# Early spectral weights loaded as row pairs, with two modes on partitions of opposite parity

## The chip, the cores and the metric

One Trainium2 chip, of which the kernel uses one core. The metric is device time in microseconds of one execution of the whole program. The core has TensorE (PE, matmuls), VectorE (DVE), ScalarE (ACT), GpSimd (POOL, which here mainly issues loads), SyncE (SP) and 16 DMA engines that carry every transfer between HBM and the on-chip SBUF. Matmul results land in PSUM, eight banks of 2 KB on each of 128 partitions.

## The reference

Attention with a forget gate, then a spectral mixing layer:

```
scores = (q @ k.T) / sqrt(64) + cum[i] - cum[j]      # cum = cumsum(log f), causal
attn   = softmax(scores);  x = attn @ v              # q, k, v: (8, 8, 576, 64) f32
x      -> (8, 576, 512)                              # heads side by side
X = rfft(x, axis=1)[:, :64]                          # 64 modes
Yr = Xr @ w_r - Xi @ w_i;  Yi = Xr @ w_i + Xi @ w_r  # per mode, w_r, w_i: (64, 512, 512) f32
y = irfft(Y, 576);  u = x + y
out = u + relu(u @ w_ch)                             # (8, 576, 512) f32
```

The two weight tensors are 134 MB together and each element is used once for each of eight batch entries. They are most of what is read.

## The kernel before

**The order.** The kernel is written under a manual schedule: each engine runs its instructions in program order. A loop of 34 turns does the attention of 32 items (four pairs of heads, `g`, by eight batch entries, `b`; item `i` is `pairs[i]`, so items 0 to 7 have `g` = 0, 8 to 15 have `g` = 1). A turn `i` holds, for item `i`, the transposes of q and k (`trans`), of v (`turn_v`, `back_v`), the scores and their exponentials on ScalarE (`scores`, lines 457 and 464), the masks; for item `i-1` the products with v (`av`, line 505) and the normalisation into `x_all` (`norm`, line 520); for item `i-2` the spectrum (`dft`). Behind the loop stands the weight stage: for each unit of four modes the remaining weight tiles are multiplied with the spectrum, and the inverse transform and the output product follow.

**The loads.** GpSimd issues q, k, v and the weights in one queue; the load casts f32 to bf16. Each turn `i` issues q and k of item `i+4`, half a weight tile (`issue_half`), v of item `i+3`, and, but in turns 3, 6, 9, 12 and 15 (`less`), another half. A weight tile has 1 MB (bf16): four modes of one unit `u`, and a quarter `dc` of the work of these modes. It sits in a rotating pool of seven buffers (`NW`), or, for a few early tiles (`guests`), in space that is not yet used. A tile's load must wait until the matmuls of the tile that had its buffer are done. The order is `wseq`: the 28 tiles of `early`, then the rest by unit.

**Two layouts of weights.** For the first eight units (`NL`, 32 modes `ML`) and the first 256 rows of the 512 (`dc` 0 and 1, 128 rows each), a tile holds w_r and w_i of four modes with one weight row on one partition (`by_rows`). One packet of such a load writes one row: 512 bf16 elements, 1 KB. In all other tiles one partition holds a pair of adjacent rows, `2p` and `2p+1`, so that one packet writes 2 KB; for the units from eight on, `dc` 0 is w_r and `dc` 1 is w_i of the first 256 rows, `dc` 2 and 3 the same of the last 256.

**The spectrum.** `dft` multiplies a block of `x_all` (time by 128 channels) with `bas3`, a basis of three planes (minus sine, cosine, sine; written by `setup_basis` in turn 1). A partition of the result is a channel. For `g` 0 and 1 it makes three groups of five matmuls: all 128 channels with the first 32 modes, which are copied to `XS`, and even channels and odd channels with the last 32 modes, on 64 partitions each, which are copied to `XQ` (by row pair). Both copies are on ScalarE (lines 543 and 547). For `g` 2 and 3 two groups make even and odd channels with all modes for `XP`.

**The early products.** `spec_early` multiplies the tiles of `early` inside the loop: two in each of turns 10 to 13, two in turn 17 behind `dft`, two in each of 18 and 19, and one in each turn from 20. `spec_mms` issues eight matmuls of 512 columns (line 221) for a tile, each with 32 (or 16) columns of spectrum as the stationary operand, and puts mode `j` into rows 32`j` to 32`j`+31 of the PSUM tile, so that four of them work on four column strips of the array. The result goes to `yacc` in `yx` by a ScalarE copy (`dc` 0) or a VectorE sum. In the weight stage `Yb` is brought to rows by a matmul with `perm`.

**PSUM.** `psM`, two buffers, is shared in order by the transposes, `pd` of `dft`, and the early products.

Of the kernel before, what the change touches and what calls it, by code (L numbers as in the profile page):

```python
# [10 lines left out]
F32 = mybir.dt.float32  # L11
BF16 = mybir.dt.bfloat16
I32 = mybir.dt.int32
ALU = mybir.AluOpType
ACT = mybir.ActivationFunctionType
# [8 lines left out]
def kernel(  # L24
# [11 lines left out]
    nc = tc.nc  # L36
    B, H, S, Dh = q.shape
    NM = moe_w_r.shape[0]
    D = H * Dh
    assert S == 576 and Dh == 64 and D == 512 and H == 8, (B, H, S, Dh)  # L40
    assert NM == 64 and B == 8
    NSB = 5
    SBLK = [128, 128, 128, 128, 64]
    NEB = D // 128
# [7 lines left out]
    NX = 12  # L52
    NL = 8
    ML = 4 * NL
    XROW = 24 * ML + 32
    scale = 1.0 / math.sqrt(Dh)
    TWO_PI_OVER_S = 2.0 * math.pi / S
    NEAREST = 1.5 * 2.0**23
# [5 lines left out]
    const = ctx.enter_context(tc.tile_pool(name="const", bufs=1))  # L64
    wpool = ctx.enter_context(tc.tile_pool(name="wpool", bufs=NW))

    yx = const.tile([128, 8, 1280], F32, name="yx")
    x_all = const.tile([128, NEB, B, NSB, 128], BF16, name="x_all")
    XS = const.tile([128, 2, XROW], BF16, name="XS")
    XP = const.tile([128, 2, 24, NM], BF16, name="XP")  # L70
    XQ = const.tile([128, 2, 24, NM - ML], BF16, name="XQ")
    wch = const.tile([128, NEB, D], BF16, name="wch")
    ident_bf = const.tile([128, 128], BF16, name="ident_bf")
    ident_f = const.tile([128, 128], F32, name="ident_f")
    trimask = const.tile([128, 128], BF16, name="trimask")
    tri4 = const.tile([128, 2, 64], BF16, name="tri4")
    perm = const.tile([128, 64], BF16, name="perm")
    Zt = const.tile([128, NSB, NM, 2], F32, name="Zt")
    bas3 = const.tile([128, NSB, 3, NM], BF16, name="bas3")
# [3 lines left out]
    wT = const.tile([128, NPAIR, 9], BF16, name="wT")  # L83
    wn = const.tile([128, NPAIR, 9], F32, name="wn")
    coef = const.tile([128, 1], F32, name="coef")
    accT = const.tile([128, NEB, B, 8], F32, name="accT")


    actx = ExitStack()
    ssb = actx.enter_context(tc.tile_pool(name="ssb", bufs=1))  # L90
# [10 lines left out]
    psM = actx.enter_context(tc.tile_pool(name="psM", bufs=2, space=PSUM))  # L101
# [44 lines left out]
    def by_rows(u, dc):  # L146

        return dc < 2 and u < NL

    def issue_w(half=None):  # L150
        n = wissued[0]
        if n >= len(wseq):
            return
        u, dc = wseq[n]
        if half != 1:
            if n in guests:
                t = 2 if by_rows(u, dc) else 4
                w8 = guests[n][:, 0 : 8 * D].rearrange("p (t m e) -> p t m e", t=t, e=D)
            else:
                shape = [128, 2, 4, D] if by_rows(u, dc) else [128, 4, 2, D]  # L160
                w8 = wpool.tile(shape, BF16, tag="w8", name="w8")
            wtile[(u, dc)] = w8
        w8 = wtile[(u, dc)]
        if by_rows(u, dc):
            for t, src in enumerate((moe_w_r, moe_w_i)):
                if half in (None, t):
                    nc.gpsimd.dma_start(
                        w8[:, t, :, :],
                        src[4 * u : 4 * u + 4, dc * 128 : (dc + 1) * 128, :].rearrange("m p e -> p m e"),
                    )  # L170
        elif dc < 2:
            src = (moe_w_r, moe_w_i)[dc]
            step = 4 if half is None else 2
            for j in range(2 * (half or 0), 4 if half != 0 else 2, step):
                m = 4 * u + j
                nc.gpsimd.dma_start(
                    w8[:, j : j + step, :, :].rearrange("p m r e -> p m (r e)"),
                    src[m : m + step, 0:256, :].rearrange("m (p r) e -> p m (r e)", r=2),
                )
        elif half != 1:  # L180
            src = (moe_w_r, moe_w_i)[dc - 2]
            step = 1 if n + 1 == len(wseq) else 4
            for j in range(0, 4, step):
                m = 4 * u + j
                nc.gpsimd.dma_start(  # L185
                    w8[:, j : j + step, :, :].rearrange("p m r e -> p m (r e)"),
                    src[m : m + step, 256:512, :].rearrange("m (p r) e -> p m (r e)", r=2),
                )
        if half != 0:
            wissued[0] += 1  # L190
# [7 lines left out]
    XPv = XP[:].rearrange("p r c m -> p (r c) m")  # L198
    XQv = XQ[:].rearrange("p r c m -> p (r c) m")

    def by_pair(dc, c, n, m):

        c0 = 24 * c + (8 if dc % 2 == 0 else 0)
        if dc < 2:
            return XQv[:, c0 : c0 + n, m - ML]
        return XPv[:, c0 : c0 + n, m]

    def spec_mms(A, u, dc, first, last):
        w8 = wtile.pop((u, dc))
        for n in range(2):  # L210
            for j in range(4):
                m = 4 * u + j
                st_, sp_ = first and n == 0, last and n == 1
                if by_rows(u, dc):
                    M = 32
                    c0 = m * 24 + (8 if n == 0 else 0)
                    lhsT, rhs = XS[:, dc, c0 : c0 + 32], w8[:, n, j, :]
                else:
                    M = 32 if st_ else 16
                    lhsT, rhs = by_pair(dc, n, M, m), w8[:, j, n, :]  # L220
                nc.tensor.matmul(  # L221
                    A[32 * j : 32 * j + M, :], lhsT=lhsT, rhs=rhs, start=st_, stop=sp_
                )

    def spec_cols(AT, dc, modes=range(4)):
# [19 lines left out]
    cum, ones1 = yx[:BH, 1, 0 : 2 * S + 64], yx[:BH, 5, 0:S]  # L245

    s_i = ssb.tile([128, NSB], I32, name="s_i")
    m_i = ssb.tile([128, 128], I32, name="m_i")
    nc.gpsimd.iota(s_i[:], pattern=[[128, NSB]], base=0, channel_multiplier=1)
    nc.gpsimd.iota(m_i[:], pattern=[[1, 128]], base=0, channel_multiplier=0)  # L250
    nc.sync.dma_start(ft, f.rearrange("b h s -> (b h) s"))
    for i in range(3):
        load_v(i, nc.sync)
# [8 lines left out]
    s_f = ssb.tile([128, NSB], F32, name="s_f")  # L262
    m_f = ssb.tile([128, 128], F32, name="m_f")
    nc.vector.tensor_copy(s_f[:], s_i[:])
    nc.vector.tensor_copy(m_f[:], m_i[:])
    nc.vector.tensor_scalar(ident_bf[:], m_f[:], s_f[:, 0:1], None, ALU.is_equal)
    nc.vector.tensor_scalar(s_f[:], s_f[:], float(S - 1), None, ALU.min)
    sm = tmpC.rearrange("p t s m -> p t (s m)")
# [61 lines left out]
        nc.vector.tensor_copy(tri4[64:128, 1, :], trimask[64:128, 64:128])  # L330

    def setup_basis():
        nc.vector.tensor_scalar(bas3[:, :, 0, :], Zt[:, :, :, 1], -1.0, None, ALU.mult)
        nc.vector.tensor_copy(bas3[:, :, 1, :], Zt[:, :, :, 0])
        nc.vector.tensor_copy(bas3[:, :, 2, :], Zt[:, :, :, 1])

    def setup_late():
        nc.vector.memset(XS[:, :, 24 * ML : XROW], 0.0)
        nc.vector.tensor_copy(
            perm[:].rearrange("p (b j ri) -> p b j ri", b=8, j=4),  # L340
            ident_bf[:].rearrange("p (j x ri b) -> p b j x ri", j=4, x=2, ri=2)[:, :, :, 0, :],
        )
        nc.vector.tensor_copy(rep[:], _strided(ident_bf[:, KF:128], [[0, 4], [1, KL]]))
        nc.gpsimd.dma_start(wch[:], moe_w_ch.rearrange("(eb p) e -> p eb e", p=128))
# [182 lines left out]
    def dft(i):  # L527
        g, b = pairs[i]
        if g < 2:
            pd = psM.tile([128, 3, 3, ML], F32, tag="m", name="pd")  # L530
            half = slice(64 * g, 64 * g + 64)
            for r in range(3):
                for sc in range(NSB):
                    ns = SBLK[sc]
                    xs = x_all[:ns, g, b, sc, :]
                    nc.tensor.matmul(  # L536
                        pd[half, r, :, :] if r else pd[:, 0, :, :],
                        lhsT=xs[:, r - 1 : 128 : 2] if r else xs,
                        rhs=bas3[:ns, sc, :, ML:NM] if r else bas3[:ns, sc, :, 0:ML],
                        start=(sc == 0),  # L540
                        stop=(sc == NSB - 1),
                    )
            nc.scalar.copy(
                XS[:, g, 0 : 24 * ML].rearrange("p (m c b) -> p c m b", c=3, b=8)[:, :, :, b],
                pd[:, 0, :, :],
            )
            nc.scalar.copy(
                XQ[half, :, :, :].rearrange("p r (c b) m -> p r c b m", c=3)[:, :, :, b, :],
                pd[half, 1:3, :, :],
            )  # L550
            return
        pd = psM.tile([128, 2, 3, NM], F32, tag="m", name="pd2")
        half = slice(64 * (g - 2), 64 * (g - 2) + 64)
        for r in range(2):
            for sc in range(NSB):
                ns = SBLK[sc]
                nc.tensor.matmul(  # L557
                    pd[half, r, :, :],
                    lhsT=x_all[:ns, g, b, sc, r:128:2],
                    rhs=bas3[:ns, sc, :, :],  # L560
                    start=(sc == 0),
                    stop=(sc == NSB - 1),
                )
        nc.scalar.copy(
            XP[half, :, :, :].rearrange("p r (c b) m -> p r c b m", c=3)[:, :, :, b, :], pd[half]
        )
# [94 lines left out]
    with ExitStack() as bctx:  # L661
# [44 lines left out]
        with ExitStack() as mctx:  # L706
# [128 lines left out]
            for u in range(NU):  # L835
                last = u == NU - 1
# [230 lines left out]
```

## Time and profile before

| | us |
|---|---|
| median of 3 runs (435.5 to 436.37) | 435.57 |
| the profiled execution | 436.07 |
| its span | 434.2 |
| PE busy | 360.4 (83%) |
| VectorE busy | 265.7 (61%) |
| ScalarE busy | 229.0 (53%) |
| GpSimd busy | 141.0 (32%) |

96.79 MB are written by DMA in 60,289 packets; HBM reads are 163.73 MB. Of the packets, 25,088 have between 512 bytes and 2 KB. The mean granted clock of TensorE is 0.947 of full speed. The loop of 34 turns takes from about 1 to 233 us, the weight stage until about 402 us, the output steps the rest.

The page divides the span into 40 slices of 10.9 us; in these rows a digit is a tenth and a 9 means 90% or more. In the timeline a line gives start, length, engine, source line, operation, output and input with their shapes, and in brackets the idle time of the engine ahead of it with what ended it. In the table of stretches the columns are the stretch, its length, the busy time of PE, its weight loads, VectorE, ScalarE and GpSimd (with the number of instructions), the granted clock, the mean share of the DMA engines (over 1 where packets overlap) and GB/s written.

### The profile page before, as it was taken

The page shows a single profiled execution, that of the slowest core. Times are in us where ns is not written, and L with a number is a line of the kernel's source. Part 1 is how long each engine was busy: PE and PEld are TensorE (multiplying, and loading weights), DVE is VectorE, ACT ScalarE, POOL GpSimd, SP SyncE. Part 2 cuts the span into 40 slices and gives each one's busy share as a digit, 9 for nine tenths or more (in the row PEclk, how much of TensorE's full clock was granted, in tenths as well). Part 3 has the DMA queues.
Part 4 walks back from the last instruction along what each step waited for, and adds up shares of the span by engine and source line. Part 5 has one row for each costly group of instructions (what it writes and reads, how often), then busy time and mean ns, then how long its engine had stood idle before and what let it go on. Part 6 is the DMA issues. An engine that isn't in the chain of part 4 may idle for free.

```text
span 434.2 us, 10695 instructions
## 1 busy us (share of the span) xinstructions
PE 360.4 (83%) x4433; PEld 200.9 (46%) x4444; DVE 265.7 (61%) x651; ACT 229.0 (53%) x374; POOL 141.0 (32%) x211
## 2 busy tenths in 40 slices
PE   1699999988898899999986386599788599989993
PEld 1466666655665565665653133244343233334330
DVE  6687888776878797787785122222323157654794
ACT  4656667677775567667661022033313176652783
POOL 6544445434544434444304101111111112001273
PEclk9999999999999999999999579599969699999997
DMA  9999999999999999999999999999999999996598
GB/s 193 205 234 220 232 222 232 226 229 230 231 231 228 230 230 230 230 230 229 236 214 212 212 212 212 212 213 212 212 212 212 212 212 212 211 212 126 188 381 305
DMA packets 60289, 96.79 MB, mean 223 GB/s; under 512 B 3664, under 2 KB 28752, under 8 KB 60240
## 3 DMA queue, kind: packets, MB, share of 16 engines
q0 software_dynamic: 54544, 85.63, 103.6%
q1 hardware_dynamic: 5696, 10.47, 6.7%
q8 instruction: 35, 0.57, 0.5%
q14 instruction: 14, 0.11, 0.1%
HBM read 163.73 MB, written 9.44 MB: 399 GB/s over the span
## 4 chain that ended last, share of the span: by engine, by line
DMA 49%; PE 31%; DVE 9%; ACT 5%; issue 3%; POOL 1%; DVEq 0%; ACTq 0%; POOLq 0%
DMA w<-in_moe_w_i_dram 34%; DMA w<-in_moe_w_r_dram 13%; PE pd L536 5%; PE pav L505 5%; PE sps L457 5%; DVE qkT L382 4%; PE tv L404 3%; ACT et L464 2%; PE A L221 2%; PE pd L557 2%; DVE vT L406 2%; PE tp L377 2%; DMA qk<-in_k_dram 2%; DVE x_all L520 2%; PE U L692 2%
## 5 line engine op out<-in xcount | busy, mean ns | idle before, releaser
L464 ACT ACTIVATE et<-sps 128x1024 bf16<-128x1024 f32 x96 | 93.2, 1023 | 11.6 <-PE sps L457 9.7
L505 PE MATMUL pav<-vs,et 128*128 128x65 bf16 (+1 forms) x896 | 51.3, 197 | 14.6 <-ACT e L451 14.3
L505 PEld LDWEIGHTS <-et 128*128 128x128 bf16 (+1 forms) x896 | 39.9, 103 | 34.0 <-issue 31.7
L382 DVE COPY qkT<-tp 128x640 bf16<-128x640 bf16 x64 | 48.9, 765 | 3.4 <-PE tp L377 3.4
L892 DVE TENSOR_TENSOR Yb<-A,yx 128x512 bf16<-128x512 f32 x15 | 10.4, 692 | 59.0 <-PE A L221 59.0
L406 DVE COPY vT<-tv 128x576 bf16<-128x576 bf16 x32 | 24.2, 757 | 35.4 <-PE tv L404 34.7
L732 PE MATMUL pxw<-wch,xT 128*128 128x512 bf16 (+1 forms) x152 | 41.1, 418 | 1.0 <-DVE xT L722 0.4
L457 PE MATMUL sps<-qkT 64*128 64x512 bf16 (+4 forms) x320 | 39.4, 310 | 1.3 <-DVE qkT L382 1.1
L426 ACT COPY vs<-vp 128x576 bf16<-128x576 bf16 x32 | 20.4, 639 | 37.1 <-PE vp L422 37.1
L520 DVE TENSOR_TENSOR x_all<-pav,rcp 128x384 bf16<-128x384 f32 (+2 forms) x96 | 36.2, 377 | 3.3
L221 PE MATMUL A<-w,XP 128*16 128x512 bf16 (+1 forms) x240 | 21.3, 435 | 20.2 <-DMA w<-in_moe_w_i_dram 12.1
L377 PE MATMUL tp<-ident_bf,qk 128*64 128x128 bf16 x576 | 30.1, 235 | 9.3 <-DMA qk<-in_k_dram 9.0
L185 POOL DMA_DIRECT2D w<-in_moe_w_r_dram x16 | 11.9, 743 | 74.6 <-PE A L221 69.2
L739 ACT CAST XW<-pxw 128x512 bf16<-128x512 f32 (+1 forms) x16 | 9.4, 585 | 45.2 <-PE pxw L732 45.2
L739 ACT CAST yx<-pxw 128x512 bf16<-128x512 f32 (+1 forms) x24 | 14.0, 585 | 33.9 <-PE pxw L732 33.9
L782 ACT CAST x_all<-pu 128x512 bf16<-128x512 f32 (+1 forms) x40 | 23.4, 585 | 13.1 <-PE pu L775 12.2
L112 POOL DMA_DIRECT2D qk<-in_q_dram x32 | 19.5, 609 | 30.8 <-PE tp L377 6.5
L185 POOL DMA_DIRECT2D w<-in_moe_w_i_dram x19 | 13.3, 698 | 50.0 <-PE A L221 40.5
L732 PEld LDWEIGHTS <-xT 128*128 128x128 bf16 (+1 forms) x160 | 15.8, 109 | 22.9 <-issue 9.6
L722 DVE COPY xT<-ptr 128x576 bf16<-128x576 bf16 x32 | 14.7, 458 | 17.8 <-PE ptr L717 17.0
L112 POOL DMA_DIRECT2D qk<-in_k_dram x32 | 19.2, 601 | 19.1 <-DMA w<-in_moe_w_i_dram 5.9
L377 PEld LDWEIGHTS <-qk 128*64 128x64 bf16 x576 | 19.5, 116 | 12.7 <-issue 8.2
(158 smaller groups left out, 703.3 us busy)
## 6 DMA issues: line engine op xcount, KB each, us to landing
w<-in_moe_w_i_dram POOLq DMA_DIRECT2D x19, 1024.0 KB, 31.9
w<-in_moe_w_r_dram POOLq DMA_DIRECT2D x16, 1024.0 KB, 29.9
w<-in_moe_w_r_dram POOLq DMA_DIRECT2D x23, 512.0 KB, 11.3
w<-in_moe_w_i_dram POOLq DMA_DIRECT2D x19, 512.0 KB, 11.0
out_dram<-o_sb SPq DMA_DIRECT2D x36, 256.0 KB, 2.8
vt<-in_v_dram POOLq DMA_DIRECT2D x29, 288.0 KB, 10.4
qk<-in_q_dram POOLq DMA_DIRECT2D x32, 144.0 KB, 10.7
qk<-in_k_dram POOLq DMA_DIRECT2D x32, 144.0 KB, 10.7
```

Of the source, the lines that this page charges most:

```text
L112: nc.gpsimd.dma_start(qk[64 * n : 64 * n + 64, :, :], src[b, 2 * g : 2 * g + 2, :, :].rearrange("h (p r) d -> p h (r d)", p=64),)
L185: nc.gpsimd.dma_start(w8[:, j : j + step, :, :].rearrange("p m r e -> p m (r e)"), src[m : m + step, 256:512, :].rearrange("m (p r) e -> p ...
L221: nc.tensor.matmul(A[32 * j : 32 * j + M, :], lhsT=lhsT, rhs=rhs, start=st_, stop=sp_)
L377: nc.tensor.transpose(tp[64 * hp : 64 * hp + 64, r - r0, :, :].rearrange("p n c -> p (n c)"), qk[:, hp, r * 64 : r * 64 + 64], ident_bf[:, :],
L382: nc.vector.tensor_copy(st[i]["T"][:].rearrange("p n (c r) -> p n c r", r=9)[:, :, :, r0:r1], tp[:, 0 : r1 - r0, :, :].rearrange("p r n c ...
L406: nc.vector.tensor_copy(st[i]["vT"][:].rearrange("p (c r) -> p c r", r=9), tv[:].rearrange("p r c -> p c r"))
L457: nc.tensor.matmul(ps[:, hp, c : c + n], lhsT=KT[sl, jb * 128 : jb * 128 + 128], rhs=QT[sl, i0 : i0 + n], start=True, stop=True,)
L464: nc.scalar.activation(st[i]["et"][:, T, :, :], ps[:], ACT.Exp, scale=scale)
L505: nc.tensor.matmul(pav[:Ms, sb % 3, hp, :], lhsT=eblk(i, hp, jb, sb), rhs=rhs, start=(jb == 0), stop=(jb == sb),)
L520: nc.vector.tensor_tensor(x_all[:ns, g, b, lo:hi, :].rearrange("p s (h d) -> p s h d", h=2), pav[:ns, lo % 3 : lo % 3 + n, :, 0:Dh], _stri ...
L732: nc.tensor.matmul(pxw[rows, :], lhsT=xT[:, eb, sb * 128 : sb * 128 + Ms], rhs=wch[:, eb, :], start=(eb == 0), stop=(eb == NEB - 1),)
L739: nc.scalar.copy(XW[to][rows, sb, :], pxw[rows, :])
```

## The change

Four things change together.

- The `by_rows` tiles hold row pairs. Partition `2q+h` holds the adjacent rows `2q`, `2q+1` (of the 128) of the modes `2h` and `2h+1` of the unit: even partitions carry two modes, odd partitions the other two. One packet writes 2 KB. For the units from eight on, `dc` 0 and 1, a half of a tile is now 128 rows on the 64 partitions of one parity (`g`), all four modes, instead of two modes of 256 rows.
- `dft` for `g` 0 and 1 makes shifted spectra: `x_all` lies in `x_pad` behind 32 zero columns, and the stationary operand starts at the block's first channel, one later, or one earlier, so that partition `p` holds channel `p`, `p+1` or `p-1`. The columns of `bas3` are reordered, with the first 32 modes in two groups of 16 around the last 32. The groups have 64, `cut` and 64-`cut` modes (`cut` 48 for `g` 0, 16 for `g` 1) on three planes: 192, 144 and 48 columns, or 192, 48 and 144.
- The copies out of PSUM multiply with a parity mask `odd` (one column is 1 on partitions of one parity, the other on the rest), so that zeros stand where a partition's mode group does not belong. For each of these spectra there are two scaled copies on ScalarE to `by_mode` (`XS`, or space in `yx` for `g` 1), and, for `g` 0, a third to `XQ`; for `g` 1 two VectorE instructions add to `XQ` what `g` 0 left.
- `spec_mms` for these tiles issues eight matmuls of 512 columns with 64 or 48 stationary columns into the two halves of the PSUM tile. The modes stand in other strips (`at`), and `perm` and `pos` follow.

```
-                        src[4 * u : 4 * u + 4, dc * 128 : (dc + 1) * 128, :].rearrange("m p e -> p m e"),
+                        w8[:, 2 * t : 2 * t + 2, :, :].rearrange("p k r e -> p k (r e)"),
+                        src[4 * u : 4 * u + 4, dc * 128 : (dc + 1) * 128, :].rearrange(
+                            "m (p r) e -> p m (r e)", r=2
+                        ),
...
-            step = 4 if half is None else 2
-            for j in range(2 * (half or 0), 4 if half != 0 else 2, step):
...
+            for g in range(2):
+                if half in (None, g):
+                    nc.gpsimd.dma_start(
+                        w8[g:128:2, :, :, :].rearrange("p m r e -> p m (r e)"),
+                        src[4 * u : 4 * u + 4, 128 * g : 128 * g + 128, :].rearrange(
...
+        if by_rows(u, dc):
+            for t in (1, 0):
+                for r in range(2):
+                    for k in range(2):
+                        M = 64 if t else 48
+                        c0 = 56 * (2 * u + k) + (0 if t else 8)
+                        nc.tensor.matmul(
+                            A[64 * k : 64 * k + M, :],
+                            lhsT=by_mode(dc)[:, r, c0 : c0 + M],
+                            rhs=w8[:, 2 * t + k, r, :],
+                            start=first and t == 1 and r == 0,
+                            stop=last and t == 0 and r == 1,
+                        )
+            return
...
     def setup_basis():
-        nc.vector.tensor_scalar(bas3[:, :, 0, :], Zt[:, :, :, 1], -1.0, None, ALU.mult)
-        nc.vector.tensor_copy(bas3[:, :, 1, :], Zt[:, :, :, 0])
-        nc.vector.tensor_copy(bas3[:, :, 2, :], Zt[:, :, :, 1])
+        nc.vector.tensor_reduce(
+            odd[:], ident_f[:].rearrange("p (q h) -> p h q", h=2), mybir.AxisListType.X, ALU.add
+        )
+        nc.vector.memset(x_pad[:, 0:32], 0.0)
...
+        for c, ri in enumerate((1, 0, 1)):
+            to, z = bas3[:, :, c, :], Zt[:, :, :, ri]
+            for o, f in [(to[:, :, 16:48], z[:, :, ML:NM])] + [
...
     def dft(i):
         g, b = pairs[i]
         if g < 2:
-            pd = psM.tile([128, 3, 3, ML], F32, tag="m", name="pd")
...
+            pd = psM.tile([128, 3, 2 * NM], F32, tag="m", name="pd")
+            even, odds, upper = (16, 0, 32) if g == 0 else (48, 32, 0)
+            cut = 16 if g else 48
+            for o, m0, m1, at in (
+                (0, 0, NM, even),
+                (1, 0, cut, NM + even),
+                (-1, cut, NM, 0),
+            ):
                 for sc in range(NSB):
...
+                    M = 127 if o == 1 and sc == NSB - 1 else 128
+                    c0 = 32 + ((g * B + b) * NSB + sc) * 128 + o
                     nc.tensor.matmul(
-                        pd[half, r, :, :] if r else pd[:, 0, :, :],
-                        lhsT=xs[:, r - 1 : 128 : 2] if r else xs,
-                        rhs=bas3[:ns, sc, :, ML:NM] if r else bas3[:ns, sc, :, 0:ML],
+                        pd[:M, :, at : at + m1 - m0],
+                        lhsT=x_pad[:ns, c0 : c0 + M],
+                        rhs=bas3[:ns, sc, :, m0:m1],
...
-            nc.scalar.copy(
-                XS[:, g, 0 : 24 * ML].rearrange("p (m c b) -> p c m b", c=3, b=8)[:, :, :, b],
-                pd[:, 0, :, :],
-            )
-            nc.scalar.copy(
-                XQ[half, :, :, :].rearrange("p r (c b) m -> p r c b m", c=3)[:, :, :, b, :],
-                pd[half, 1:3, :, :],
-            )
+            pr = pd[:].rearrange("p c (r m) -> p r c m", r=2)
+            for h, k in enumerate((even, odds)):
+                nc.scalar.activation(
+                    by_mode(g)[:, :, 0 : XROW - 8].rearrange("p r (q c) -> p r c q", c=56)[
+                        :, :, 32 * h + b : 32 * h + 24 : 8, :
+                    ],
+                    pr[:, :, :, k : k + 16],
+                    ACT.Copy,
+                    scale=odd[:, h : h + 1],
+                )
+            xq = XQ[:].rearrange("p r (c b) m -> p r c b m", c=3)[:, :, :, b, :]
+            up = pr[:, :, :, upper : upper + 32]
+            if g == 0:
+                nc.scalar.activation(xq, up, ACT.Copy, scale=odd[:, 0:1])
+            else:
+                for r in range(2):
+                    nc.vector.scalar_tensor_tensor(
+                        xq[:, r], up[:, r], odd[:, 1:2], xq[:, r], ALU.mult, ALU.add
+                    )
```

## The prediction

> **What bounds the kernel now.** I read the slices of the page first, then the stretches by engine, the chain, one turn of the attention loop in the timeline, and last the GpSimd queue where that loop ends.
>
> ```profile
> DMA  9999999999999999999999999999999999996598
> GB/s 193 205 234 220 232 222 232 226 229 230 231 231 228 230 230 230 230 230 229 236 214 212 212 212 212 212 213 212 212 212 212 212 212 212 211 212 126 188 381 305
> ```
> ```profile
> 60.00:80.00 20.00, 18.69 (x346) 13.07 (x344) 16.74 (x47) 14.49 (x24) 8.95 (x15) 1.00 1.21 230
> 240.00:260.00 20.00, 13.43 (x82) 5.53 (x83) 4.06 (x8) 2.92 (x5) 2.22 (x3) 0.61 1.12 212
> ```
> The DMA engines are full from about 20 to 400 us: no slice falls before the outputs begin. The GB/s are bytes written; a bf16 weight is read as four bytes, so 212 GB/s are 424 GB/s read. The end is set by this stream and a tail of some 33 us. The second thing to see is that PE (first number) is at 18.7 of 20 us in the loop and at 13.4 in the weight stage: the loop is nearly as tight as the stream.
>
> One turn of the loop (the columns are start, length, engine, line), and the same copies in a later turn:
>
> ```profile
> 57.94 1.37 PE L536 MATMUL pd<-bas,x_all 128*128 128x96 bf16 x15
> 59.34 0.60 ACT L543 CAST XS<-pd 128x96 bf16<-128x96 f32 x1 [0.71 <-PE pd L536]
> 59.48 0.61 ACT L547 CAST XQ<-pd 64x192 bf16<-64x192 f32 x1
> 59.99 2.98 ACT L464 ACTIVATE et<-sps 128x1024 bf16<-128x1024 f32 x3
> 62.87 0.22 ACT L451 ACTIVATE e<-pav 128x64 bf16<-128x64 f32 x1
> 63.14 0.28 PE L505 MATMUL pav<-vs,et 128*64 128x65 bf16 x4 [0.39 <-ACT e L451]
> ...
> 92.18 0.61 PE L221 MATMUL A<-w,XS 128*32 128x512 bf16 x8
> 92.28 0.60 ACT L543 CAST XS<-pd 128x96 bf16<-128x96 f32 x1 [0.97 <-PE pd L536]
> 92.90 0.31 ACT L547 CAST XQ<-pd 64x192 bf16<-64x192 f32 x1
> ```
> It is a closed ring of 6.2 us: the spectrum matmuls, two copies of them on ScalarE, three exponentials, the small one, the last products, and the next spectrum matmuls at 64.14. ScalarE has no idle time in it but the wait for pd. What is added to the copies or to pd lengthens the turn.
>
> The GpSimd queue at the loop's end:
>
> ```profile
> 216.15 0.74 POOL L185 DMA_DIRECT2D w<-in_moe_w_r_dram  x1 [5.05 <-PE AT L233]
> 222.66 0.74 POOL L185 DMA_DIRECT2D w<-in_moe_w_i_dram  x1 [5.77 <-PE A L221]
> 228.94 0.74 POOL L185 DMA_DIRECT2D w<-in_moe_w_r_dram  x1 [5.53 <-PE A L221]
> 231.76 0.74 POOL L185 DMA_DIRECT2D w<-in_moe_w_i_dram  x1 [2.08 <-PE A L221]
> ```
> ```profile
> 216.15 20.84 DMA w<-in_moe_w_r_dram
> ```
> Here a load waits for a weight buffer, and the buffer for an early unit's product in the loop. So a loop that ends later issues these loads later. The stream has a cover: the load of 216.15 lands at 236.99, and one tile (1 MB at 212 GB/s) lands every 4.95 us, so that of 228.94 lands at 246.9. Alone it would need 2.4 us from issue to first packet (the first load: issued 1.39, first packet 3.78), 4.95 of data and about 2 until it counts as landed (that load again), 9.3 in all. It could be issued at 237.6 without being late: **a cover of 8.7 us**; counting the work still queued instead gives 7. For the loads of 216.15, 222.66 and 231.76 the same working gives 11.6, 10 and 10.9, so 8.7 decides.
>
> **The change, part by part.** The sum is made against the profiled execution, 436.07 us (span 434.2), 0.5 over the median 435.57.
>
> *Transfers.* 16,384 packets of 1 KB become 8,192 of 2 KB. Counting the trace's packets in stretches of 20 us from 20 to 380 us and solving for the engine time of each size gives 79.5 ns for 1 KB and 155.4 for 2 KB: a pair goes from 159.0 to 155.4. 8,192 x 3.6 ns / 16 engines = 1.85 us (1.2 to 2.5 by the fit's spread). This is all that the transfers can bring. The skill's page "DMA: Bandwidth & Descriptors" (the Trainium skill, section Specifications) puts line rate at 512 B and more, by which the gain would be nothing and the best outcome no change; the 2% above lean slightly against it. The units from eight on keep 2 KB packets; their halves go to 64 partitions of one parity. q and k rows already go to 64 partitions, at 93 ns for 1,152 B by the same fit, the pace of the others, so I take no cost. On GpSimd's queue four whole tiles (the imaginary parts of the last units) become two issues each: 4 x 0.7 us beside 109.6 us of waiting for PE, hidden. SP's queue is not touched.
>
> *Setup of the basis (turn 1, on VectorE, which has no gap there).* Three conversions at 0.39 us apart (0.47 each, 320 elements) become nine of 160 and 80, with one reduction and six fills (a fill of 32 words took 0.085). By 0.2 a conversion, 0.3 the reduction and 0.1 a fill: 2.7 less 1.2, some +1.2 net of overlap (0.5 to 2).
>
> *Spectrum matmuls.* Fifteen of 96 columns (1.37 us, spaced 40 ns, with two changes between 128 and 64 rows in each group of five) become five of 192, five of 144, five of 48. The groups of 192 in the later spectra are spaced 80 ns. So +40, +20 and -20 ns for five each, less the floor of some 27 ns at 48: **+0.15 us** (0.1 to 0.3 if weights read from an odd column load slower).
>
> *Copies, first eight spectra.* XS and XQ let the exponentials start 0.65 us after pd. After: two copies of 96 scattered elements to 128 partitions with a scale read per partition, then XQ. The nearest row for the scattered one is XS, 0.60; on the 128-partition side copies follow one another (92.28, 92.90). So 0.6 + 0.6 + 0.3 = 1.5, +0.85. Less 0.13 by which the third exponential waits for PE anyway, plus 0.15 of pd: +0.86 a turn (0.25 to 1.15), **6.9 us in eight turns** (2 to 9.2). The low bound is the row of 59.34 and 59.48, where a copy starts 0.14 after the other. The Trainium skill, "ScalarE: Activation LUTs", section What ACT_TABLE_LOAD costs, gives an ACTIVATE as 186 ns and 0.833 ns an element, 93 ns more for a scale by pointer, 93 ns of overlap: an estimate of 0.36 for a scattered copy. XS itself, without pointer, took 0.60, so the trace does not agree for such a destination; by the page the whole sum would be 10 us in place of 16 and the time about 437.
>
> *Early products.* Eight matmuls of 32 columns run four beside each other: two waves, 0.55 us to the next instruction. With 64 output rows each, two run beside each other (the q/k transposes, alternating halves, show two at 28 ns a matmul of 128 columns): four waves of 0.22, **+0.45 each**, sixteen of them. Turns 10 to 13 have two: behind pd the whole 0.45, ahead of pd 0.2, since there PE waits 0.24 for ScalarE; with pd's 0.15, +0.8 a turn, 3.2 (2.2 to 4.5). Turn 17 has two directly behind the last pd and waited 0.7 for XS: now for two copies, 0.9 + 0.6 + 0.15 = 1.65 (1 to 1.8). Turns 18 and 19: 0.65 each, 1.3; 20 and 21: 0.45 each, 0.9.
>
> *Second eight spectra.* ScalarE's 0.92 us (92.28 to 93.21) becomes two copies, 1.2; the rest goes to VectorE as two sums of 96 elements, some 0.25 each. They wait for pd; behind them stands vT, for which VectorE idles 0.82 to 2.4 us: hidden (without that cover 0.5 a turn). In turns 14 to 16: 0.15 + 0.28, 1.3 together (0.4 to 1.6). In 10 to 13 PE is the longer side, counted.
>
> Sum of the loop's delay: 1.2 + 6.9 + 3.2 + 1.3 + 1.65 + 1.3 + 0.9 = **16.4 us** (8 to 21). From turn 22 on nothing changes and nothing in the loop waits for a load, so it arrives whole at the loads of 216 to 232. Less the cover, 16.4 - 8.7 = **+7.7 us** of idle DMA. The 1.85 is swallowed: the stream only waits the earlier. PE, then 8.7 late against the data, catches up: it idles some 20 us between 220 and 280. What is late next are the weight tiles; the tail is as before. 436.07 + 7.7 = 443.8, at the median 443.3; I say **443**.
>
> **Rivals.**
> 1. *Faster: the loop's delay stays under the cover.* It decides at 8.7 us. For it: the low ends of the copies (2 us) and of the setup already give 8 to 9; against it: XS at 0.60 in sixteen of sixteen and the ring without slack. The end then moves with the transfers: 435.57 - 1.85 = 433.7.
> 2. *The copies pipeline* as XS and XQ do at 59.34: three in 0.9 us. Then the first eight turns cost 2.0, turns 14 to 16 0.45, turn 17 1.05; the sum is 10.1, less 8.7: +1.4, 437.0. Against it: at 92.28 they don't. The page named above would be this case.
> 3. *Reloads of ScalarE's table*, if the scaled copy were not in the table of the exponential: a load took 1.28 us (three in the whole run), two a spectrum, 41 us more: 16.4 + 41 - 8.7, about 484. Against: Relu ran behind the exponentials without one.
> 4. *The packets gain nothing.* The forecast stays, since the loop decides; case 1 becomes no change.
>
> **Numbers.** Forecast (its own range 439.5 to 449.5, from 12.5 to 22.5 us of delay) 0.62; rival 1 0.17; rival 2 (435 to 439) 0.18, of which a third lies within 0.2%; rival 3 0.03; rival 4 takes 0.02 of rival 1's to no change. 0.2% (0.9 us) is about what three runs of this kernel tell from nothing. Faster 0.17 (rival 1 without 4, and the lowest edge of 2), same 0.08, slower 0.75. The range 433.7 to 447.5 leaves out rival 3, the upper end of the forecast (0.1) and the lower half of rival 1 (some 0.06).
>
> **What would show it.** Right: turns of the first eight spectra at about 7 us in place of 6.2, two scaled copies of 0.6; early products of eight at 1.0; the loads now at 216 to 229 some 16 us later, and a fall of GB/s between 215 and 250; the 212 GB/s stage unchanged behind it. Wrong: copies 0.3 long; or a full DMA row throughout, the end then 2 us earlier; or turns that grow elsewhere, as by a wait of pd for its PSUM buffer. The forecast rests most on the copies (6.9 of 16.4) and on the cover: 3 us less of one or more of the other halve the loss.

## The result and the profile after

The changed kernel takes 448.73 us (median of 5 runs, 447.73 to 450.92), the kernel before beside it 436.09: a ratio of 1.0285, 95% interval 1.0254 to 1.0317. The profiled execution is one of 448.73 us with a span of 446.9. The forecast was 443.0, its range ended at 447.5.

The slices of the page of the changed kernel, each 11.2 us:

```profile
DMA  8999999999997499999999899999999999999498
GB/s 193 208 236 222 236 232 232 231 235 236 226 207 150 90 219 237 222 237 225 234 226 183 148 208 212 212 212 212 212 212 212 212 212 211 211 212 202 164 381 307
```

Two holes stand where the row of before had none: one at 123 to 157 us (207, 150, 90), the other at 235 to 257 (183, 148). The second is the one that the prediction looked for, at the end of the loop. The first it did not have. From 268 us on the rows are those of before (212). In stretches (columns as before: PE, weight loads, VectorE, ScalarE, GpSimd, clock, DMA share, GB/s):

```profile
60.00:80.00 20.00, 17.68 (x302) 12.12 (x300) 16.20 (x46) 14.31 (x24) 8.86 (x14) 1.00 1.13 233
120.00:140.00 20.00, 17.45 (x307) 11.97 (x306) 17.12 (x52) 13.76 (x22) 5.85 (x10) 1.00 0.91 184
140.00:160.00 20.00, 12.97 (x143) 6.83 (x141) 7.73 (x21) 7.22 (x10) 6.05 (x10) 0.83 0.71 134
240.00:260.00 20.00, 15.83 (x228) 9.40 (x231) 13.89 (x42) 6.14 (x10) 5.93 (x8) 0.99 0.94 163
```

Between 140 and 160 us PE is idle for 7 of the 20 us, and VectorE, ScalarE and GpSimd for more than half of them. The timeline of the changed kernel says why (start, length, engine, line, and in brackets the idle time ahead of it with what ended it):

```profile
135.37 0.64 POOL L177 DMA_DIRECT2D yx<-in_moe_w_r_dram  x1 [8.67 <-ACT yx L597]
...
143.88 1.12 ACT L597 ACTIVATE yx<-pd,odd 128x96 bf16<-128x96 f32 x2 [4.28 <-DMA yx<-in_moe_w_r_dram]
...
145.05 3.62 PE L233 MATMUL A<-w,yx 128*64 128x512 bf16 x16 [4.67 <-ACT yx L597]
...
149.94 0.65 POOL L177 DMA_DIRECT2D yx<-in_moe_w_r_dram  x1 [11.56 <-issue]
...
159.88 1.29 DVE L645 TENSOR_TENSOR yx<-A,yx 128x512 f32<-128x512 f32 x2 [4.07 <-DMA yx<-in_moe_w_r_dram]
```

Weight tiles 16 and 17 of the load order, the real parts of units 8 and 9, are guests: they go to `yx`, tile 16 to rows 4 and 5, tile 17 to rows 6 and 7. In the changed kernel `yx` also holds the second spectra (rows 5 and 7, behind column 768) and, as before, the early sums (rows 0 to 3 at this time). None of these shares a byte with the tiles. Still, the load of tile 16 waits 8.67 us until ScalarE has copied the spectrum of turn 16; ScalarE's copies of turn 17 then wait for that load to land; PE waits for the copies; tile 17's load waits 11.56 us, until the sums of turn 17 are done (the second ended at 149.41; the profile names no releaser for this wait, so that it is the sums is read from the times here and from the kernel with the spectra out of `yx` below); and the sums of turn 18 wait for tile 17 to land. GpSimd's queue is in order, so behind the two waiting loads stand q, k, v and the next weights. That is the first hole.

The start of the small exponential of each turn (line 451 before, 497 after) gives the loop's delay against the kernel before:

| | forecast | after | after, turns 17 to 19 as without the waits |
|---|---|---|---|
| setup of the basis and first eight spectra | 8.1 | 4.5 | 4.5 |
| turns 10 to 13 | 3.2 | 2.0 | 2.0 |
| turns 14 to 16 | 1.3 | 0.6 | 0.6 |
| turn 17 | 1.65 | 7.4 | 1.6 |
| turns 18 and 19 | 1.3 | 5.3 | 1.1 |
| turns 20 and 21 | 0.9 | 0.9 | 0.9 |
| sum | 16.4 | 20.7 | 10.7 |

The last column takes turns 17 to 19 from two experiments below in which these waits are gone or without effect (9.20, 8.39 and 8.39 us from one small exponential to the next, against 15.00, 11.31 and 9.65 here, and 7.61, 7.83 and 7.83 before; the expectations below number these turns by the exponential that ends them, 18 to 20): the waits are 5.8 + 2.9 + 1.3 = 10.0 us of the 20.7. The delay is whole at the loop's end, where the loads come late by it:

```profile
229.86 0.74 POOL L188 DMA_DIRECT2D w<-in_moe_w_i_dram  x1 [5.76 <-PE A L247]
236.77 0.74 POOL L188 DMA_DIRECT2D w<-in_moe_w_r_dram  x1 [6.17 <-PE AT L259]
243.28 0.74 POOL L188 DMA_DIRECT2D w<-in_moe_w_i_dram  x1 [5.77 <-PE A L247]
251.27 0.74 POOL L188 DMA_DIRECT2D w<-in_moe_w_r_dram  x1 [7.25 <-PE pav L551]
```

The load that stood at 216.15 stands at 236.77. Of 20.7 us of delay 12.66 (448.73 less 436.07, the profiled executions) are lost at the end, so 8.0 were covered.

One turn of the first eight spectra, timeline of the changed kernel:

```profile
60.17 1.58 PE L588 MATMUL pd<-bas,x_pad 128*128 128x192 bf16 x15
...
61.79 1.12 ACT L597 ACTIVATE XS<-pd,odd 128x96 bf16<-128x96 f32 x2 [0.82 <-PE pd L588]
62.40 0.66 ACT L608 ACTIVATE XQ<-pd,odd 128x192 bf16<-128x192 f32 x1
62.97 2.84 ACT L510 ACTIVATE et<-sps 128x1024 bf16<-128x1024 f32 x3
...
65.67 0.24 ACT L497 ACTIVATE e<-pav 128x64 bf16<-128x64 f32 x1
```

The turn is 6.69 us in place of 6.20. The spectrum's matmuls take 1.58 (1.37 before), and from the first copy to the exponentials it is 1.18 us (0.65 before).

### The profile page after: what moved, and what is told of

It is laid out like the page before. It is cut to its first block, busy times and chain, and to the rows that moved or that the text cites. A ratio compares the mean times of both kernels' runs of the same rounds, so it can differ in the third digit from the quotient of the medians.

```text
span 446.9 us, 10746 instructions
## 1 busy us (share of the span) xinstructions
PE 371.4 (83%) x4433; PEld 206.2 (46%) x4444; DVE 271.2 (61%) x679; ACT 233.5 (52%) x382; POOL 139.6 (31%) x215
## 4 chain that ended last, share of the span: by engine, by line
DMA 38%; PE 13%; issue 11%; POOL 2%; DVE 2%; ACT 1%; DVEq 0%; POOLq 0%
DMA w<-in_moe_w_i_dram 20%; DMA w<-in_moe_w_r_dram 16%; DMA yx<-in_moe_w_r_dram 2%; PE U L755 2%; PE Z L755 2%; POOL w L188 1%; PE U L1020 1%; PE A L233 1%; PE pav L551 1%; PE pd L620 1%; PE A L247 1%; PE sps L503 1%; PE tp L423 0%; PE tv L450 0%; PE pywl L1039 0%
## 5 line engine op out<-in xcount | busy, mean ns | idle before, releaser
L551 PE MATMUL pav<-vs,et 128*128 128x65 bf16 (+1 forms) x896 | 51.7, 198 | 13.7 <-ACT e L497 13.4
L503 PE MATMUL sps<-qkT 64*128 64x512 bf16 (+4 forms) x320 | 40.3, 315 | 1.6 <-DVE qkT L428 1.1
L795 PE MATMUL pxw<-wch,xT 128*128 128x512 bf16 (+1 forms) x152 | 39.6, 406 | 1.0 <-DVE xT L785 0.4
L566 DVE TENSOR_TENSOR x_pad<-pav,rcp 128x384 bf16<-128x384 f32 (+2 forms) x96 | 36.2, 377 | 3.5
L845 ACT CAST x_pad<-pu 128x512 bf16<-128x512 f32 (+1 forms) x40 | 23.4, 584 | 13.3 <-PE pu L838 12.5
L588 PE MATMUL pd<-bas,x_pad 128*128 128x192 bf16 (+7 forms) x240 | 25.3, 225 | 0.5 <-DVE qkT L428 0.4
L440 DVE TENSOR_TENSOR vn<-vt,wn 128x576 bf16<-128x576 f32 x32 | 23.8, 743 | 2.4 <-ACT wn L345 2.4
```

The costliest lines, as they stand in the source:

```text
L440: nc.vector.tensor_tensor(vn[:], st[i]["vt"][:], _strided(wn[:, widx(i), :], [[1, 9], [0, Dh]]), ALU.mult)
L503: nc.tensor.matmul(ps[:, hp, c : c + n], lhsT=KT[sl, jb * 128 : jb * 128 + 128], rhs=QT[sl, i0 : i0 + n], start=True, stop=True,)
L551: nc.tensor.matmul(pav[:Ms, sb % 3, hp, :], lhsT=eblk(i, hp, jb, sb), rhs=rhs, start=(jb == 0), stop=(jb == sb),)
L566: nc.vector.tensor_tensor(x_all[:ns, g, b, lo:hi, :].rearrange("p s (h d) -> p s h d", h=2), pav[:ns, lo % 3 : lo % 3 + n, :, 0:Dh], _stri ...
L588: nc.tensor.matmul(pd[:M, :, at : at + m1 - m0], lhsT=x_pad[:ns, c0 : c0 + M], rhs=bas3[:ns, sc, :, m0:m1], start=(sc == 0), stop=(sc == N ...
L795: nc.tensor.matmul(pxw[rows, :], lhsT=xT[:, eb, sb * 128 : sb * 128 + Ms], rhs=wch[:, eb, :], start=(eb == 0), stop=(eb == NEB - 1),)
```

## The experiments

All were measured beside the kernel before, at 435.8 to 436.1 us.

**How much delay is covered.** The kernel before, with the first group of matmuls of each of the first sixteen spectra issued once or twice more, which delays the loop and touches nothing else:

```
-            for r in range(3):
+            for r in [0] * 1 + [0, 1, 2]:
```

> The kernel before, with the first group of five spectrum matmuls issued twice in each of the sixteen early spectra (the result is the same): nothing but a loop that is later, by about 0.4 us a turn, 6.5 us in all. Theory A (a delay of the loop costs nothing up to a cover of about 8 us, and one for one beyond): no change, 435.5 to 436.8. Rival C (no such cover; a delay costs what it is): 442 to 443.

It takes 435.98 us (ratio 0.9991, 0.9973 to 1.0008), with a delay of 5.8 us at the loop's end. With `[0] * 2`:

> As the one before, with the group issued three times: the loop is later by about 0.8 us a turn, 13 us in all. Theory A: 13 less 8 to 8.7, so 4.3 to 5 us over the kernel before, 440 to 441.5. Rival C: 449. Were the stream to hide it all, 436.

It takes 441.11 us (1.0108, 1.0049 to 1.0167), with a delay of 13.2. The timeline of the second shows what was added, 25 matmuls where there were 15, and its slices show the hole of the loop's end alone:

```profile
60.97 2.21 PE L536 MATMUL pd<-bas,x_all 128*128 128x96 bf16 x25
```
```profile
GB/s 192 205 234 219 233 221 232 233 227 228 231 232 224 212 223 226 224 238 223 238 195 163 188 211 211 212 212 212 212 212 212 212 212 212 212 213 163 181 367 315
```

So 5.8 us of delay cost nothing and 13.2 cost 5.0: the cover is near 8 us. From 13.2 to the changed kernel's 20.7 the delay grows by 7.5 and the loss by 7.7: past the cover the delay is paid one for one.

**The row pairs alone.** The kernel before, with only the load of the first eight units' tiles as row pairs; the products then multiply rows with the wrong channels:

```
-                        w8[:, t, :, :],
-                        src[4 * u : 4 * u + 4, dc * 128 : (dc + 1) * 128, :].rearrange("m p e -> p m e"),
+                        w8[:, t, :, :].rearrange("p (k r) e -> p k (r e)", r=2),
+                        src[4 * u : 4 * u + 4, dc * 128 : (dc + 1) * 128, :].rearrange(
+                            "m (p r) e -> p m (r e)", r=2
+                        ),
```

> The kernel before, with only the loads of the first eight units' first 256 rows changed to row pairs of 2 KB; the matmuls are left as they were, so that they multiply the wrong rows. It shows what the transfers alone bring. From the fit of the packets (159.0 to 155.4 ns for a pair): 1.85 us faster, 433.8 to 434.7, with the loop as before. If 1 KB packets cost no more than 2 KB ones by the byte: no change.

434.11 us (0.9946, 0.9927 to 0.9966): the pairs bring 2.0 us, where the loop is not delayed. The fit of the packets had given 1.85.

**The second spectra out of `yx`.** They get a tile of their own, over the space of `Zt`, which is not read any more by then; their gaps are zeroed in turn 9, and the small `accT` takes free columns of `yx`, so that all fits.

```
-        return yx[:, 5:8:2, 768 : 768 + XROW // 2].bitcast(BF16)
+        return XS1
```

> The changed kernel, but the spectrum of the second 128 channels (by_mode(1)) lies in the space of Zt, which is free by then, instead of in yx beside two guest tiles; accT, used only at the end, moves into yx for room. Theory A (in the changed kernel the loads of the guest tiles into yx and the ScalarE copies into yx wait for each other, some 10 us of the loop's 20.7 us of delay): GpSimd's waits of 8.7 and 11.6 us at 127 to 150 us vanish, turns 18 to 20 fall from 15.0, 11.3 and 9.7 to 8 to 9.3 us, the loop ends 10 to 11.5 us late instead of 20.7, and with a cover of 8 the time is 2 to 3.5 us over the kernel before: 438 to 440. Rival B (the waits are only the loop's own 7 us of delay having used up the early loads' slack): the waits stay, the time stays at 447 to 449.

441.76 us (1.0119, 1.0082 to 1.0156), delay 11.8. The wait of 8.67 is gone, that of tile 17 is not, and here the profile names the sum as its releaser (timeline, tiles 16 and 17):

```profile
127.28 0.64 POOL L179 DMA_DIRECT2D yx<-in_moe_w_r_dram  x1 [0.35 <-issue]
...
144.41 0.64 POOL L179 DMA_DIRECT2D yx<-in_moe_w_r_dram  x1 [11.98 <-DVE yx L649]
```

The theory held for one of the two loads. What tile 17 waits for now is a sum into row 0 of `yx`, which it shares no row with, and which the kernel before also made, without a wait. The place of the spectra was therefore not the whole cause. What had changed besides is how the guests are written: a half is 128 rows on the partitions of one parity, every second partition, where it had been two modes on all 128.

**The guests written to blocks of partitions.** The changed kernel, with the halves of tiles 16 and 17 on partitions 0 to 63 and 64 to 127, and nothing else:

```
-                        w8[g:128:2, :, :, :].rearrange("p m r e -> p m (r e)"),
+                        (w8[64 * g : 64 * g + 64, :, :, :] if n in (16, 17) else w8[g:128:2, :, :, :]).rearrange(
+                            "p m r e -> p m (r e)"
+                        ),
```

> The changed kernel, except that the two halves of the tiles 16 and 17, the two that go to space in yx, are written to partitions 0 to 63 and 64 to 127 in place of the partitions of one parity. Bytes and packets are the same; the product of these two units then multiplies the wrong rows. Theory A (two causes: the write to every second partition of yx is taken to touch everything in yx, so tile 16 waits for any copy or sum in yx; and the spectra's place in rows 5 to 7 of yx is taken with what lies between, so tile 17 and the spectrum copies wait for each other): the load of tile 16 is issued near 127.3 us without the wait of 8.7, tile 17 waits only for the copies of turn 16 (near 135 to 138), and the copies of turn 17 wait for tile 17 to land; the loop's delay falls from 20.7 to some 13 to 17 us, the time to 440 to 445. Theory B (the place of the spectra in yx alone makes all waits): nothing changes, tile 16 still waits 8.7 us and the time is 448 to 449. Theory C (the write to every second partition alone): all waits go, the delay is 10 to 11 us, the time 438 to 439.

438.98 us (1.0065, 1.0044 to 1.0086), delay 10.9.

```profile
128.46 0.62 POOL L177 DMA_DIRECT2D yx<-in_moe_w_r_dram  x1 [0.77 <-DMA vt<-in_v_dram]
...
142.12 0.63 POOL L177 DMA_DIRECT2D yx<-in_moe_w_r_dram  x1 [7.69 <-ACT yx L599]
```

Tile 16 no longer waits for the spectra, though these still lie in `yx`. Tile 17 still waits 7.69 us for them (the spectra's two rows, 5 and 7, reach over its rows 6 and 7). So theory A is right that there are two causes. But its load stands behind the copies of turn 17 in the order of the program, and not ahead of them as theory A had it, so no copy waits for it, and the time is that of theory C. Theory B is out. The part of tile 17 was priced too dear: its late load costs nothing at the end.

**Both.** The spectra in their own tile, and `yx` as two tiles of four rows, so that sums and guests are apart:

```
-    yx = const.tile([128, 8, 1280], F32, name="yx")
+    ya = const.tile([128, 4, 1280], F32, name="ya")
+    yb = const.tile([128, 4, 1280], F32, name="yb")
```

> The changed kernel with the second spectra in a tile of their own and yx as two tiles of four rows each, so that the early sums (rows 0 to 3) and the tiles 16 and 17 (rows 4 to 7) share no tile. Theory A (with the tile of its own alone, what was left was tile 17's wait of 12.0 us for a sum): tile 17 is issued near 132 to 138 us, DMA stays full between 120 and 160, turns 18 to 20 take 8.3, 8.8 and 8.7 us, the loop's delay at the end is 10 to 11 us in place of 11.9, and less a cover of 8 the time is 438 to 439. Rival: the wait of 12.0 cost nothing in the end, since DMA can be given its work later; then 441.8 stays.

439.51 us (1.0108, 1.0070 to 1.0146), delay 11.4 (0.5 of it from a later start of the loop).

```profile
128.27 0.64 POOL L184 DMA_DIRECT2D yb<-in_moe_w_r_dram  x1 [0.35 <-DMA vt<-in_v_dram]
...
134.98 0.64 POOL L184 DMA_DIRECT2D yb<-in_moe_w_r_dram  x1 [1.68 <-DMA w<-in_moe_w_i_dram]
```

Neither load waits for a spectrum or a sum, and the turns in question take 9.19, 8.38 and 8.39 us (8.3, 8.8 and 8.7 expected). The time is that of the kernel with blocks, within the spread, and half a us above the range I gave. So of the changed kernel's 448.73 us the tile for the spectra takes away 7.0, the blocks 9.75, and the tile with `yx` in two 9.2; they don't add up, they take away the same thing: a load to every second partition of `yx` was ordered against everything in `yx`. That the program keeps such a write as one range over all columns is my reading of these four runs; the trace shows the waits, not the rule that made them.

**What the copies cost.** The kernel with `yx` in two tiles, its scaled copies writing 48 adjacent elements in place of steps of eight and 56, so that the first eight units multiply spectra in the wrong order:

```
-                    by_mode(g)[:, :, 0 : XROW - 8].rearrange("p r (q c) -> p r c q", c=56)[
-                        :, :, 32 * h + b : 32 * h + 24 : 8, :
-                    ],
+                    by_mode(g)[:, :, 96 * b + 48 * h : 96 * b + 48 * h + 48].rearrange(
+                        "p r (c q) -> p r c q", c=3
+                    ),
```

> The kernel with yx in two tiles, except that the two scaled copies of the first sixteen spectra write 48 elements in a row each in place of steps of eight; what the first eight units multiply is then in the wrong order. Theory S (the scattered destination is what the copies cost: 0.69 us each, 1.18 us from the first copy to the exponentials against 0.65 before): the copies take 0.3 to 0.4 us, the turns of the first eight spectra fall from 6.69 to 6.4 us or less, the delay at the end from 11 to 8 or 9 us and the time from 439.5 to 436 to 438. Rival P (the copies follow one another before they end, so their length counts little, and pd and the number of copies set the turn): the turns stay at 6.6 to 6.7 and the time at 439 to 440.

435.82 us (0.9998, 0.9980 to 1.0017). The groups of ScalarE, first of the kernel with scattered copies, then of the dense one (busy time, mean ns of one, idle before):

```profile
L606 ACT ACTIVATE XS<-pd,odd 128x96 bf16<-128x96 f32 x16 | 9.0, 790 | 7.0 <-PE pd L597 7.0
...
L617 ACT ACTIVATE XQ<-pd,odd 128x192 bf16<-128x192 f32 x8 | 5.3, 661 | 0.0
```
```profile
L603 ACT ACTIVATE XS<-pd,odd 128x96 bf16<-128x96 f32 x16 | 4.6, 337 | 7.8 <-PE pd L594 7.8
L614 ACT ACTIVATE XQ<-pd,odd 128x192 bf16<-128x192 f32 x8 | 3.4, 422 | 0.0
```

A copy of the same 96 elements takes 337 ns in place of 790. `XQ`, whose destination did not change, falls from 661 to 422, so a part of such a length belongs to the copies ahead; but the first copy of a turn, with no copy ahead of it, takes 341 in place of 692. The turns fall from 6.69 to 6.40 in the first eight spectra and from 6.47 to 6.04 in turns 14 to 16: theory S. The delay at the end is 9.1 us in place of 11.4. Of it 3.0 stem from ahead of the fourth exponential, against 1.5 in the scattered kernel; what made these first turns longer is not shown (the gaps are zeroed in another way, but without any such change the kernel with the row pairs alone starts its loop 1.4 us earlier than the kernel before). From there on the dense copies save 3.7. The median is 3.7 less too, and 0.2 under the range expected. With a cover of 8 a delay of 9.1 should lose 1 us: the profiled execution, whose delay this is, took 437.37, 1.3 over that of before; the median shows no loss, with 0.7 allowed by the interval.

**A longer cover.** The kernel with `yx` in two tiles, and three early products brought forward, so that the buffers that the late loads wait for come free sooner; and the same edit on the kernel before:

```
-        for _ in range({14: 0, 15: 0, 16: 0, 17: 2}.get(i, int(i >= 10))):
+        for _ in range({14: 0, 15: 0, 16: 0, 17: 2, 22: 2, 23: 2, 24: 2, 31: 0, 32: 0, 33: 0}.get(i, int(i >= 10))):
```

> As the kernel with yx in two tiles, and three early products brought forward: two in each of turns 22, 23 and 24 and none in turns 31 to 33. Each of the buffers that the loads behind the loop wait for comes free some three turns (19 us) earlier. Theory A (of the loop's delay only what exceeds the cover costs time, and the row pairs save 2.0 us of DMA): the loads issued at 228 to 242 are issued before 222 us, DMA stays full to the outputs, and the time is 433.5 to 434.5, 2 us under the kernel before. Rival (the delay costs time by itself, PE behind the data): 438 or more.

> The kernel before, with the same three early products brought forward and nothing else. Theory A: DMA was full anyway, so 435.5 to 436.5, no change. Rival (the order of the products is worth time by itself): 435 or less, and what the row pairs bring with it is less than the whole difference.

The first takes 435.63 us (0.9985, 0.9968 to 1.0002), the second 436.47 (1.0011, 0.9994 to 1.0029). The loads that the kernel with `yx` in two tiles issued at 227.6, 234.1 and 242.1 us go out at 212.5, 216.8 and 225.0, the last of them 3 us later than expected. The loop is late by 13.7 us and the time is that of before, so the rival, that the delay costs time by itself, is out, and the edit alone is worth nothing. But the 434 that I expected did not come. In its profiled run the DMA is full to the outputs and the last weight tile lands at 399.8 us (401.5 before), yet PE finishes its product 1.0 us later, not 0.45:

```profile
386.00:390.00 4.00, 2.35 (x16) 1.12 (x16) 1.86 (x5) 2.21 (x4) 0.82 (x3) 1.00 1.12 211
390.00:394.00 4.00, 4.00 (x40) 2.02 (x41) 1.38 (x3) 1.17 (x2) 0.39 (x2) 0.57 1.12 211
394.00:398.00 4.00, 4.00 (x52) 2.07 (x51) 2.93 (x5) 1.17 (x2) 0.00 (x0) 1.00 0.73 137
```

PE was granted 0.57 of its clock just ahead of the end. With two products forward in place of three (`22: 2, 23: 2, 32: 0, 33: 0`):

> As the kernel with three early products brought forward, but two: two in each of turns 22 and 23 and none in turns 32 and 33, so the loads behind the loop come some 13 us earlier in place of 19. Theory A (with the loop's delay covered DMA is full to the outputs, and the time then differs only by how PE's clock stands at the end, which in the profiled run with three was granted at 0.58 from 390 to 394 us): DMA full to 390 us, the time 434 to 435.6. Rival (three was needed, since loads that wait for PE show again): a fall of GB/s between 215 and 260 us and 436 or more.

434.67 us (0.9972, 0.9959 to 0.9986), faster than both kernels. Its slices are full to the outputs, and its clock from 380 to 400 us is 1.00:

```profile
GB/s 194 207 238 222 236 222 236 236 230 231 235 234 225 236 224 232 223 234 225 239 211 212 212 212 212 212 211 212 212 212 212 212 211 212 211 211 123 214 353 309
```

Whether the clock is what parts the two versions in the median is not settled: runs of the one with three lie between 433.96 and 437.34, of the other between 434.04 and 436.30.

## The prediction, point by point

*The direction and its mechanism were right.* The loop ends later, the loads behind it are issued later by as much, the DMA runs dry at 235 to 257 us, and the stage behind is as before. Rival 1 failed: even without the waits the delay, 10.7 us, passes the cover. That the forecast's own range, up to 449.5, holds the time is luck: its 22.5 us of delay were allowed for terms other than the waits.

*The cover was right.* 8.7 forecast; the delays and losses of the runs give 8.0 (changed kernel, profiled executions: 20.7 and 12.7), 8.2 (loss by the medians: 13.2 and 5.0) and 7.8 (by the medians: 10.9 and 3.15). The kernel with the spectra in their own tile lost 5.6 us by the median and 4.8 in the profiled execution, at a delay of 11.8. That is 1 to 2 us more than a cover of 8 gives, and it stays unexplained: the kernel with blocks had the late tile 17 as well.

*The transfers were right*: 1.85 forecast, 2.0 measured (1.5 to 3.2 by the interval). They were swallowed as said: the kernels with row pairs have no longer cover (8.0 and 7.8) than the one without (8.2). The skill's page "DMA: Bandwidth & Descriptors" (the Trainium skill, Specifications) puts line rate at 512 B and more; that packets of 1 KB and 2 KB do alike, as the prediction read it, does not agree with the 2.0 us.

*The step that failed is in Transfers: "their halves go to 64 partitions of one parity ... so I take no cost".* I looked at the pace of the packets and not at who orders the write. It made loads, copies and sums in `yx` wait for each other, 10.0 us of delay and, past the cover, all of it time (448.73 against 438.98 without). "Second eight spectra" failed with it: it priced the copies to `yx` as copies and did not ask what else lives in `yx` in turn 17. The prediction named "turns that grow elsewhere" as a sign of error, but no mechanism for it; the profile of before could not show the wait, but the code could: a tile loaded into shared space, with a new pattern, while two engines write to that space.

*Copies, first eight spectra: mis-sized.* 0.86 us a turn forecast with the matmuls, 0.53 measured (3.7 over the seven turns that hold nothing else). I laid the three copies end to end, 1.5 us; their starts are 0.24, 0.38 and 0.56 apart, 1.18 from the first to the exponentials, so +0.53 and not +0.85. With +0.22 until the copies start and some 0.25 that the exponentials and the last products give back, the turn shown grew by 0.49. Rival 2 (0.9 for the three) was on the right track: 1.18 lies between it and the forecast's 1.5, and dense copies show 0.77. The estimate of 0.36 us for a copy, from the Trainium skill's "ScalarE: Activation LUTs" (What ACT_TABLE_LOAD costs), agrees with the dense copy, 0.34, and not with the scattered one, 0.79. My row for it, the scattered `XS` of before with 0.60, was the better one for the length, and wrong for the pace.

*Spectrum matmuls and setup.* The prediction's own terms for the matmuls, +40, +20 and, by its floor, -13 ns for five each, come to 0.23 us and not to the 0.15 that it wrote; 0.21 was measured. The setup was given 1.2. What it cost is not settled: the delay is 0.07 us at the third exponential and 0.75 at the fourth, behind the first of these spectra, and the runs' first turns differ by more than that.

*Early products:* 0.45 each forecast; 0.44 in turns 20 and 21, where nothing else changed. Turn 17: 1.65 forecast, 1.6. Turns 10 to 13 were given 0.8 each and cost 0.5, on PE: dense copies leave them at 8.1 us. Turns 14 to 16 were given 0.43 each and cost 0.2; there the copies decide, as the dense ones show.

So without the unseen waits the sum of 16.4 would have been 5.7 too high, and the time 439 in place of 443. Against the profiled execution the sum said 443.8 and 448.73 came, 4.9 more: 10.0 of waits that were missing, less the 5.7 that were too much, and 0.7 from the cover. Two errors partly cancel, and the range, made from the known terms alone, was too short above.

## What to carry to other kernels

When a change writes a shared tile in a new pattern (every second partition, rows with a step), list all that engines read and write in that tile at the time, and count a wait for each as if the bytes overlapped; separate tiles, or a pattern in blocks, take the waits away. Price copies by the distance of their starts in a row like them, not by their lengths, and look at the step of the destination. Where a loop feeds a stream that is the bound, the delay of the loop costs only what passes the cover, so freeing buffers two turns earlier can be worth as much as shortening the loop.

## What the runs showed of the hardware that was not expected

The step of a ScalarE copy's destination more than doubles its time: 96 bf16 elements a partition, 790 ns in steps of 16 and 112 bytes, 337 ns in rows of 48 (692 and 341 for the first copy of a turn, which has none ahead of it). The prediction had 0.6 for the former.

PE's granted clock fell to about half behind short idle times, and not in each run alike. In the changed kernel PE idled 4.67 us at 140 us, its clock from 144 to 150 us was granted at 0.50, and the sixteen matmuls behind the wait took 3.62 us. In the kernel with three products forward an idle time of 1.21 us at the same place was followed by a clock of 0.53 to 0.61 for 4 us, and the same sixteen took 3.58 us; in the kernel with `yx` in two tiles the same 1.21 us left the clock at 1.00, and they took 1.92. The Trainium skill's "TensorE: Matmul & The Clock Gate" (What's actually happening) has the clock halved behind an idle window of about 3.4 us that runs free of the program: the first case, with its 4.67 us, agrees; the second has less idle time than that, so the rule as it stands does not give it. That the same wait once does it and once does not would fit a window that runs free, but no run here shows the window.
